# First expert's opening products in two interleaved sums, and table reads ahead of weight loads

## The chip, the core and the metric

The kernel runs on one core of one Trainium2 chip. The metric is the device time of one execution in microseconds (us); less is better. The engines are named as in the profile: PE (TensorE, with PEld for its weight loads), DVE (VectorE), ACT (ScalarE), POOL (GpSimd) and SP (SyncE, whose DMA queue is shown as SPq).

## The reference: what is computed

A linear attention with decay runs over 768 steps for 4 x 8 heads. Its rows, put together as 3072 tokens of 512 values, go through a layer of 8 experts, of which each token takes one.

```python
for t in range(S):                                   # S = 768, D = 64
    state = gamma * state + einsum('bhd,bhe->bhde', k[:, :, t], v[:, :, t])
    y[:, :, t] = scale * einsum('bhd,bhde->bhe', q[:, :, t], state)
x = y.transpose(0, 2, 1, 3).reshape(3072, 512)
...
logits = xn @ en.T / tau                             # xn, en: rows of length one
expert_idx = argmax(logits, axis=1)
gate_w = softmax(logits)[n, expert_idx]
for e in range(8):
    mask = expert_idx == e
    h = maximum(x[mask] @ w1[e], 0.0)                # 512 -> 1024
    out[mask] = gate_w[mask, None] * (h @ w2[e])     # 1024 -> 512
```

## The kernel before

**The attention part** walks over 12 chunks of 256 tokens (`m` from 0 to 11). In a chunk PE makes the scores and products, `take(m)` has ACT copy the result out of the two PSUM banks `py0` and `py1` into `yT` (one copy for `py0`, two half copies for `py1`), `rows_turn` and `rows` turn it into token rows and write them to DRAM (`xd`), and `logits_products`, `sums` and `choose` find each token's expert. `count`, `ranks` and `place` give every token a place in the table `tbl` in DRAM: `place` is one indirect DMA on POOL for each block of 128 tokens. The chunks are placed in groups; the last two groups are chunks 9 and 10, and chunk 11.

**The expert part** starts with the first 288 tokens of expert 0 (`EARLY`), which are known before chunk 11 is done. They are gathered as rows (`xge`), transposed by PE in 12 transposes (four column blocks `kt`, three row groups each) into four PSUM banks, and split into two float32r parts: `xh0`, rounded by ACT, and `xl0`, the rest, by DVE. Weights are split in the same way: `load_piece` issues the load of one piece of 512 KB (eight to an expert) on SP's queue into one of four `raw` buffers, `split` has ACT write `whi` and DVE `wlo`, each with nine buffers. Each product of the first layer is then three matmuls: `xh` by `whi`, `xl` by `whi`, `xh` by `wlo`. `products` is a generator that gives one matmul of expert 0's first layer at a time, so that `run(n)` puts n of them between other steps. The accumulators come from `acc_`, which goes round the PSUM banks in a fixed order, and the other results from `pt_`, which goes round b0 to b3:

```python
return bank(("py0", "py1", "pst0", "pst1", "b0", "b1")[nacc[0] % 6])
```

So the accumulator of the first output block is the bank `py0`, that of the second is `py1`, the same two that `take(11)` copies from.

**The rest of expert 0 and expert 1.** The 128 late tokens of expert 0 and the rows of expert 1 can be gathered only once all tokens are placed. SP reads their table entries into `tb` (the statement for `tb[:, 0, 3]` and `slots(1)`), POOL gathers (`xr`), `write_rows(1)` writes expert 1's rows to DRAM (`xs`) and `read_quarters(1)` reads them back in another layout (`xg`), from which `x_turn(1, kt)` (DVE transpose, ACT rounding) and `x_low(1, kt)` (DVE) make expert 1's `xh` and `xl`. Beside that PE works on expert 0's second layer, on the late tokens' products (`hr`), on their transposes (`turn_hidden`) and second layer (`layer2_rows`), and then begins expert 1. `split` calls stand between these steps.

**Order.** The instructions of all engines run in the order in which the program writes them (a manual schedule): every engine, and SP's queue, is a list worked off from its head, and a wait holds up all that stands behind it on that engine. The pools add waits where a buffer or bank is taken again.

Of the kernel before, what the change touches and what calls it, by code (L numbers as in the profile page):

```python
# [11 lines left out]
F32 = mybir.dt.float32  # L12
# [12 lines left out]
P = 128  # L25
# [80 lines left out]
def retention_moe(ctx: ExitStack, tc: tile.TileContext, q, k, v, emb, tau, w1, w2, const, const16, out):  # L106
# [503 lines left out]
    def turn_rows(xr, jn, kt, ps=None):  # L610
        ps = pt_() if ps is None else ps
        for c, (j, n) in enumerate(jn):
            nc.tensor.transpose(ps[:, c * P:c * P + n], xr[:n, j, kt * P:(kt + 1) * P], ident[:n, :n])
        return ps

    def rows_T(xr, jn, kt, at, ps=None):

        ps = turn_rows(xr, jn, kt) if ps is None else ps
        w = at.stop - at.start
        nc.scalar.copy(out=xh0[:, kt, at], in_=ps[:, :w])  # L620
        nc.vector.tensor_tensor(out=xl0[:, kt, at], in0=ps[:, :w], in1=xh0[:, kt, at].bitcast(F32), op=ALU.subtract)  # L621
# [139 lines left out]
    for m in range(NM):  # L761
# [61 lines left out]
        else:  # L823
# [39 lines left out]
            else:  # L863
# [4 lines left out]
                for low in lows:  # L868
                    low()
                intra(m, 1)  # L870
                pr = count(done)
                ps = [turn_rows(xge, EROWS, kt, bank(f"pst{kt}")) for kt in range(2)]
                run_all(ranks(done, pr))
                place(range(span(done).start, span(done).stop))
# [9 lines left out]
        if m == NM - 1:  # L884
            for kt in range(KT):
                rows_T(xge, EROWS, kt, slice(0, EARLY), ps[kt] if kt < 2 else None)
# [11 lines left out]
    def products():  # L898
        for ft in range(FT):
            acc = acc_()  # L900
            yield from first_layer(0, ft, acc, xh0, xl0, early)
            hidden(ft, acc, hh0, hl0, early, held if ft < 2 else None)
# [12 lines left out]
    m, g = NM - 1, len(GROUPS) - 1  # L915
    pl = logits_products(m)
# [4 lines left out]
    run(11)  # L921
# [13 lines left out]
    low()  # L935
    for _ in range(9):
        next(sort_steps)
        run(1)
    load_expert(1)
    load_piece()  # L940
    run(10)
    split()
    load_piece()
    load_expert(2)
    nc.sync.dma_start(out=tb[:, 0, 3], in_=tbl[EARLY:CAPS[0], :2 + NE])
    slots(1)
    slots(2)
    run(12)
    split()
    for j, n in EROWS:  # L950
        square(xge, n, j, j)
    run(12)
    split()
    load_piece()
    load_piece()
# [157 lines left out]
    write_rows(1)  # L1113
    hr = mp.tile([P, DF], F32, name="hr")
# [14 lines left out]
    load_piece()  # L1129
    load_piece()  # L1130
# [16 lines left out]
    squares(1, 1)  # L1147
    load_piece()
# [211 lines left out]
```

## Time and profile before

| what | value |
| --- | --- |
| time, median of 3 runs (lowest to highest) | 409.28 us (408.39 to 411.97) |
| profiled execution: time | 409.33 us |
| profiled execution: span from first to last instruction | 407.6 us |
| PE busy | 392.3 us, 96% of the span |
| DVE, ACT, POOL busy | 62%, 52%, 38% of the span |
| mean granted PE clock | 0.986 |
| DMA | 88.39 MB, mean 217 GB/s |

The span is 1.7 us shorter than the time of the same execution; sums in spans are carried to the time by adding this. A PE that is busy 96% of the span says where to look for the few stretches in which it isn't, not that each matmul is at its peak.

### The profile page before, as it was taken

To read this page: it belongs to the slowest core of one execution; us is meant where nothing else is said; L and a number is where in the kernel's file an instruction comes from. 1 tells how busy PE (TensorE), PEld (TensorE's weight loads), DVE (VectorE), ACT (ScalarE), POOL (GpSimd) and SP (SyncE) were. 2 spreads that over 40 slices of the span, in tenths; PEclk is the share of its full clock that TensorE was granted. 3 is DMA by queue.
4 is the path that set the end of the run, shared out by engine and by line. 5 is a ranking of instruction groups with operands and counts; after the bars stand their busy time and mean duration, and the time that the engine had idled before them with its cause. 6 is when DMAs were issued, how large, how long until landed. Compare 5 with 4: busy or idle time off the path is not lost.

```text
span 407.6 us, 9526 instructions
## 1 busy us (share of the span) xinstructions
PE 392.3 (96%) x3646; PEld 359.1 (88%) x3646; DVE 254.2 (62%) x539; ACT 213.5 (52%) x378; POOL 154.8 (38%) x170
## 2 busy tenths in 40 slices
PE   7999999999899999999999999999999999999993
PEld 3998788878687998899999999999889889999972
DVE  5496877767489847871963676396266465586400
ACT  4565566545484627543745644565475365563410
POOL 2666477676333270701631330261274062000040
PEclk9999999999799999999999999999999999999997
DMA  8998979888437978879596896888969958934121
GB/s 233 266 291 255 270 218 261 238 220 245 112 81 189 277 233 198 282 222 276 187 297 166 254 301 197 233 280 248 257 242 329 206 183 247 247 127 126 32 98 53
DMA packets 88479, 88.39 MB, mean 217 GB/s; under 512 B 10808, under 2 KB 67000, under 8 KB 88424
## 3 DMA queue, kind: packets, MB, share of 16 engines
q1 hardware_dynamic: 83176, 74.60, 64.5%
q0 software_dynamic: 5072, 13.03, 9.4%
q8 instruction: 30, 0.49, 0.5%
q14 instruction: 25, 0.20, 0.1%
q10 hardware_dynamic: 176, 0.07, 0.1%
HBM read 65.01 MB, written 18.79 MB: 206 GB/s over the span
## 4 chain that ended last, share of the span: by engine, by line
PE 76%; DVE 6%; issue 6%; DMA 5%; SPq 4%; POOL 1%; ACT 1%; POOLq 0%; DVEq 0%; ACTq 0%
PE pst L237 11%; PE b L237 9%; PE py L237 8%; PE py L1030 8%; PE b L1030 6%; PE pst L1030 6%; PE py L444 5%; PE b L381 5%; PE b L1078 4%; PE py L1078 4%; PE pst L415 2%; SPq L1042 2%; PE b L350 2%; DMA tbl<-parts 2%; DVE x L468 2%
## 5 line engine op out<-in xcount | busy, mean ns | idle before, releaser
L224 DVE TENSOR_TENSOR wlo<-raw,whi 128x1024 fp32r<-128x1024 f32 x64 | 77.8, 1219 | 21.0 <-ACT whi L219 13.6
L1060 POOL DMA_INDIRECT out_dram<-og,si x28 | 30.4, 1086 | 125.1 <-ACT og L1053 88.7
L219 ACT CAST whi<-raw 128x1024 fp32r<-128x1024 f32 x64 | 66.2, 1044 | 2.1 <-DMA raw<-in_moe_w_dram 2.1
L1011 DVE STREAM_TRANSPOSE xt<-xg 128x384 f32<-128x384 f32 (+1 forms) x28 | 15.7, 579 | 34.1 <-DMA xg<-xs 33.9
L596 POOL DMA_INDIRECT xr<-xd,gi x24 | 29.9, 1244 | 17.2 <-ACT sq L278 9.9
L401 DVE TENSOR_TENSOR pm<-b,mask 128x512 f32<-128x512 f32 x48 | 29.8, 681 | 9.1 <-PE b L381 9.1
L344 POOL TENSOR_TENSOR hl<-wlo,cst 128x512 f32<-128x512 f32 x22 | 22.7, 1051 | 32.9 <-DMA wlo<-in_k_dram 20.9
L237 PE MATMUL pst<-xl,whi 128*128 128x380 f32 (+7 forms) x96 | 32.1, 335 | 0.2 <-issue 0.2
L237 PE MATMUL pst<-xh,whi 128*128 128x380 f32 (+7 forms) x96 | 32.0, 334 | 0.0
L237 PE MATMUL pst<-xh,wlo 128*128 128x380 f32 (+7 forms) x96 | 32.0, 333 | 0.0
L566 POOL DMA_INDIRECT tbl<-zt,sloti x24 | 24.4, 1018 | 19.2 <-DVE sloti L557 8.9
L381 PE MATMUL b<-qT,kT 64*128 64x128 f32 x384 | 27.9, 283 | 2.9 <-issue 2.0
L1012 ACT CAST xh<-xt 128x408 fp32r<-128x408 f32 (+6 forms) x28 | 14.3, 510 | 28.4 <-DVE xt L1011 27.4
L381 PEld LDWEIGHTS b<-qT,kT 64*128 64x128 f32 x384 | 24.0, 187 | 5.6 <-issue 3.8
L237 PE MATMUL py<-xl,whi 128*128 128x288 f32 (+7 forms) x80 | 26.3, 328 | 0.5 <-DVE xl L621 0.5
L237 PE MATMUL b<-xh,whi 128*128 128x408 f32 (+7 forms) x80 | 26.7, 334 | 0.0
L237 PE MATMUL b<-xl,whi 128*128 128x408 f32 (+7 forms) x80 | 26.7, 333 | 0.0
L237 PE MATMUL b<-xh,wlo 128*128 128x408 f32 (+7 forms) x80 | 26.6, 332 | 0.0
L237 PE MATMUL py<-xh,whi 128*128 128x288 f32 (+7 forms) x80 | 26.3, 329 | 0.0
L237 PE MATMUL py<-xh,wlo 128*128 128x288 f32 (+7 forms) x80 | 26.2, 328 | 0.0
L444 PE MATMUL py<-pm,vs 128*64 128x128 f32 x384 | 24.3, 277 | 0.3 <-DVE vs L394 0.3
L243 ACT ACTIVATE hh<-pst 128x380 fp32r<-128x380 f32 (+7 forms) x24 | 11.6, 484 | 23.8 <-PE pst L237 23.1
(222 smaller groups left out, 1036.5 us busy)
## 6 DMA issues: line engine op xcount, KB each, us to landing
raw<-in_moe_w_dram SPq DMA_DIRECT2D x60, 512.0 KB
whi<-in_q_dram SPq DMA_DIRECT2D x24, 256.0 KB
xd<-x SPq DMA_DIRECT2D x48, 128.0 KB
wlo<-in_k_dram SPq DMA_DIRECT2D x11, 512.0 KB
xs<-xr SPq DMA_DIRECT2D x6, 768.0 KB
whi<-in_v_dram SPq DMA_DIRECT2D x6, 512.0 KB
wlo<-in_v_dram SPq DMA_DIRECT2D x6, 512.0 KB
xg<-xs SPq DMA_DIRECT2D x16, 192.0 KB
```

Of the source, the lines that this page charges most:

```text
L219: nc.scalar.copy(out=hv, in_=rv)
L224: eng.tensor_tensor(out=lv, in0=rv, in1=hv.bitcast(F32), op=ALU.subtract)
L237: nc.tensor.matmul(acc[:, :w], a[:, f], x[:, kt, cols], start=(n == 0), stop=(n == 3 * KT - 1))
L344: return eng.tensor_tensor(out=ks_r[:, m % 3, s, h], in0=kin[m % 3][:, h, s], in1=w[:, h], op=ALU.mult)
L381: nc.tensor.matmul(psc[a][:, j], kTs[m][a * D:(a + 1) * D, j, u].rearrange("p s c -> p (s c)"), q_cols(m, a, j, u), start=True, stop=True, ...
L401: o.append(nc.vector.tensor_tensor(out=pm, in0=psc[a], in1=w, op=ALU.mult))
L444: nc.tensor.matmul(pys[m][u][o * D:(o + 1) * D, j], lhsT, rhs, start=first, stop=True, skip_group_check=True)
L566: i = nc.gpsimd.indirect_dma_start(out=tbl[:, :], out_offset=bass.IndirectOffsetOnAxis(ap=sloti[:, n:n + 1], axis=0), in_=zt[:, n], in_off ...
L596: return nc.gpsimd.indirect_dma_start(out=xr[:n, j, :], out_offset=None, in_=xd[:rows_, :], in_offset=bass.IndirectOffsetOnAxis(ap=gi[:n, ...
L1030: nc.tensor.matmul(acc[:, :c], a[:, f], x[:, kt, :c], start=(n == 0), stop=(n == 3 * FT - 1))
L1060: i = nc.gpsimd.indirect_dma_start(out=out[:, :], out_offset=bass.IndirectOffsetOnAxis(ap=si[:n, e, j:j + 1], axis=0), in_=og[:n, j, :], i ...
L1078: nc.tensor.matmul(acc[:s, :], x[:, kt, at], a, start=(n == 0), stop=(n == 3 * FT - 1))
```

## The change: what it does

Four things are changed together, between the end of chunk 11 and the start of expert 1.

1. **Transposes and copies.** The 12 transposes of `xge` go row group by row group over all four banks, ahead of `count`, and the four roundings to `xh0` are put on ACT ahead of `take(11)`. On DVE the four subtractions to `xl0` now come ahead of the last `wlo` and of `ranks`, so that `place` of that group follows them.
2. **Products.** The first two output blocks of expert 0 are summed side by side, matmul by matmul, in the order all `xh` by `whi`, all `xl` by `whi`, all `xh` by `wlo`. Twelve of these 24 matmuls come ahead of the logits of chunk 11.
3. **Table reads.** On SP the reads of `tb` for expert 0's late tokens and for expert 1 come ahead of the weight load beside them, the squares of `xge` come earlier on ACT, and three splits of expert 0's weights are spread evenly.
4. **Weight loads.** Of expert 1's pieces (8 to 15) one is loaded where four were; piece 9 follows `write_rows(1)`, pieces 10 to 12 follow `read_quarters(1)`, 13 to 15 come later.

```diff
-    def turn_rows(xr, jn, kt, ps=None):
-        ps = pt_() if ps is None else ps
+    def turn_rows(xr, jn, ps):
         for c, (j, n) in enumerate(jn):
-            nc.tensor.transpose(ps[:, c * P:c * P + n], xr[:n, j, kt * P:(kt + 1) * P], ident[:n, :n])
-        return ps
-
-    def rows_T(xr, jn, kt, at, ps=None):
-
-        ps = turn_rows(xr, jn, kt) if ps is None else ps
-        w = at.stop - at.start
-        nc.scalar.copy(out=xh0[:, kt, at], in_=ps[:, :w])
-        nc.vector.tensor_tensor(out=xl0[:, kt, at], in0=ps[:, :w], in1=xh0[:, kt, at].bitcast(F32), op=ALU.subtract)
+            for kt in range(KT):
+                nc.tensor.transpose(ps[kt][:, c * P:c * P + n], xr[:n, j, kt * P:(kt + 1) * P], ident[:n, :n])
+
+    def rows_high(kt, at, ps):
+        nc.scalar.copy(out=xh0[:, kt, at], in_=ps[:, at])
+
+    def rows_low(kt, at, ps):
+        nc.vector.tensor_tensor(out=xl0[:, kt, at], in0=ps[:, at], in1=xh0[:, kt, at].bitcast(F32), op=ALU.subtract)
...
-                for low in lows:
-                    low()
+                lows.pop(0)()
                 intra(m, 1)
+                ps = [bank(f"pst{kt}") for kt in range(2)] + [pt_(), pt_()]
+                turn_rows(xge, EROWS, ps)
                 pr = count(done)
-                ps = [turn_rows(xge, EROWS, kt, bank(f"pst{kt}")) for kt in range(2)]
-                run_all(ranks(done, pr))
-                place(range(span(done).start, span(done).stop))
+                for kt in range(KT):
+                    rows_high(kt, slice(0, EARLY), ps[kt])
         waiting = done
         take(m)
...
         if m == NM - 1:
             for kt in range(KT):
-                rows_T(xge, EROWS, kt, slice(0, EARLY), ps[kt] if kt < 2 else None)
+                rows_low(kt, slice(0, EARLY), ps[kt])
+            lows.pop(0)()
+            run_all(ranks(done, pr))
+            place(range(span(done).start, span(done).stop))
...
     def products():
-        for ft in range(FT):
+        accs = [acc_(), acc_()]
+        for i in range(3):
+            for kt in range(KT):
+                x = xl0 if i == 1 else xh0
+                for ft, acc in enumerate(accs):
+                    nc.tensor.matmul(acc[:, :EARLY], piece[kt][i // 2][:, ft * P:(ft + 1) * P], x[:, kt, early],
+                                     start=(i + kt == 0), stop=(i == 2 and kt == KT - 1))
+                    yield
+        for ft, acc in enumerate(accs):
+            hidden(ft, acc, hh0, hl0, early, held)
+        for ft in range(2, FT):
             acc = acc_()
             yield from first_layer(0, ft, acc, xh0, xl0, early)
-            hidden(ft, acc, hh0, hl0, early, held if ft < 2 else None)
+            hidden(ft, acc, hh0, hl0, early)
...
     m, g = NM - 1, len(GROUPS) - 1
+    run(12)
     pl = logits_products(m)
     logits_rows(m, pl)
     rows(m - 1)
     load_piece()
     load_piece()
-    run(11)
+    run(6)
...
     low()
+    for j, n in EROWS:
+        square(xge, n, j, j)
     for _ in range(9):
         next(sort_steps)
         run(1)
+    nc.sync.dma_start(out=tb[:, 0, 3], in_=tbl[EARLY:CAPS[0], :2 + NE])
     load_expert(1)
-    load_piece()
-    run(10)
-    split()
+    slots(1)
     load_piece()
     load_expert(2)
-    nc.sync.dma_start(out=tb[:, 0, 3], in_=tbl[EARLY:CAPS[0], :2 + NE])
-    slots(1)
     slots(2)
-    run(12)
-    split()
-    for j, n in EROWS:
-        square(xge, n, j, j)
-    run(12)
-    split()
-    load_piece()
-    load_piece()
+    for _ in range(3):
+        run(12)
+        split()
...
     write_rows(1)
+    load_piece()
...
     read_quarters(1)
-    load_piece()
-    load_piece()
+    for _ in range(3):
+        load_piece()
...
     squares(1, 1)
+    load_piece()
     load_piece()
```

On ACT, where chunk 11 ends (`yT` is copied from `py`, `xh` from the banks of the transposes, `whi` is a weight split), the order before is:

```order
L219 CAST whi<-raw 128x1024 x2
L460 COPY yT<-py_2082 128x4x128
L463 COPY yT<-py_2083 64x4x128 x2
L620 CAST xh<-pst_2173 128x288
L620 CAST xh<-pst_2177 128x288
L620 CAST xh<-b_2205 128x288
```

and now it is:

```order
L219 CAST whi<-raw 128x1024 x2
L616 CAST xh<-pst_2166 128x288
L616 CAST xh<-pst_2167 128x288
L616 CAST xh<-b_2168 128x288
L616 CAST xh<-b_2169 128x288
L460 COPY yT<-py_2082 128x4x128
```

The copies that empty `py` (2082 and 2083 are the two banks of chunk 11) have moved from ahead of the four `xh` copies to behind them.

On PE, at the same place, the order before is (`pst` and `b` are the transposes' banks, `enT` the logits, `py_2237` the accumulator of the first output block):

```order
L613 MATMUL b_2205<-ident,xge 128x32
L613 MATMUL b_2211<-ident,xge 128x128 x2
L613 MATMUL b_2211<-ident,xge 128x32
L488 MATMUL b_2219<-yT,enT 32x256 x4
L237 MATMUL py_2237<-xh,whi 128x288
L237 MATMUL py_2237<-xl,whi 128x288
L237 MATMUL py_2237<-xh,wlo 128x288
```

and now it is, with the last matmul of `count` at its head (`py_2219` and `py_2220` are the two accumulators):

```order
L537 MATMUL b_2182<-oh,ones 128x8
L905 MATMUL py_2219<-xh,whi 128x288
L905 MATMUL py_2220<-xh,whi 128x288
...
L905 MATMUL py_2220<-xl,whi 128x288
L488 MATMUL b_2233<-yT,enT 32x256 x4
L905 MATMUL py_2219<-xl,whi 128x288
```

Twelve products, which go to both banks in turn, now stand ahead of the logits, and the transposes and `count` ahead of them.

On SP's queue, from the table reads to expert 1's rows, the order before is (`raw` are weight loads, `xs` the rows written, `xg` the rows read back):

```order
L945 DMA tb<-tbl 128x10
...
L913 DMA tb<-tbl 128x4x10
...
L194 DMA raw<-in_moe_w_dram 128x1024
L194 ISA
L194 DMA raw<-in_moe_w_dram 128x1024
L982 DMA xs_66<-xr 128x512
```

and now it is:

```order
L992 DMA xs_66<-xr 32x512
L194 ISA
L194 DMA raw<-in_moe_w_dram 128x1024
L1007 DMA xg<-xs_66 32x13x128
...
L194 ISA
L194 DMA raw<-in_moe_w_dram 128x1024
L194 ISA
L194 DMA raw<-in_moe_w_dram 128x1024
```

The loads of pieces 9, 10 and 11 have moved from ahead of expert 1's row writes to behind them, piece 9 in front of the reads `xg` and the other two behind these.

## Rows read from the trace of the kernel before

**Rows 1.** Page, part 1: busy time, share of the span, instructions.

```profile
PE 392.3 (96%) x3646; PEld 359.1 (88%) x3646; DVE 254.2 (62%) x539; ACT 213.5 (52%) x378; POOL 154.8 (38%) x170
```

**Rows 2.** What PE waited for, 130:376: us, times, longest.

```profile
PE pst L237 <- issue: 0.2, 1, 0.2
```

**Rows 3.** Timeline of PE around chunk 11's end: start, us, what, idle before.

```profile
121.94 0.19 PE L533 MATMUL b<-cum,ones 128*128 128x32 f16 x1
...
122.30 1.14 PE L613 MATMUL pst<-ident,xge 128*128 128x128 f32 x6
...
124.45 0.64 PE L488 MATMUL b<-yT,enT 128*32 128x256 f32 x8
125.02 0.40 PE L237 MATMUL py<-xh,whi 128*128 128x288 f32 x1
125.93 0.40 PE L237 MATMUL py<-xl,whi 128*128 128x288 f32 x1 [0.51 <-DVE xl L621]
126.17 0.29 PE L237 MATMUL py<-xh,wlo 128*128 128x288 f32 x1
126.30 0.29 PE L237 MATMUL py<-xh,whi 128*128 128x288 f32 x1
```

**Rows 4.** Timeline of ACT, same place.

```profile
121.19 0.58 ACT L460 COPY yT<-py 128x512 f32<-128x512 f32 x1
122.06 1.17 ACT L463 COPY yT<-py 64x512 f32<-64x512 f32 x2 [0.29 <-PE py L444]
123.25 0.70 ACT L620 CAST xh<-pst 128x288 fp32r<-128x288 f32 x2
124.01 0.94 ACT L620 CAST xh<-b 128x288 fp32r<-128x288 f32 x2
```

**Rows 5.** Timeline of DVE, same place.

```profile
122.63 2.36 DVE L224 TENSOR_TENSOR wlo<-raw,whi 128x1024 fp32r<-128x1024 f32 x2
...
125.42 0.81 DVE L621 TENSOR_TENSOR xl<-pst,xh 128x288 fp32r<-128x288 f32 x2
```

**Rows 6.** Stretches of 1.5 us: length, PE busy (instructions), granted clock, DMA share, GB/s.

```profile
103.50:105.00 1.50, 0.59 (x5) 1.00 0.83 224
...
106.50:108.00 1.50, 1.50 (x28) 0.50 0.14 38
...
112.50:114.00 1.50, 1.50 (x12) 0.76 0.00 0
```

**Rows 7.** Timeline of POOL: gathers for expert 0's late tokens and expert 1.

```profile
143.90 1.16 POOL L596 DMA_INDIRECT xr<-xd,tb  x1 [4.59 <-DMA tb<-tbl]
...
145.68 1.11 POOL L596 DMA_INDIRECT xr<-xd,gi  x1 [0.28 <-POOL gi L590]
```

**Rows 8.** Timeline of SP's queue: start of the issue, us, what.

```profile
137.48 1.00 SPq L194 DMA_DIRECT2D raw<-in_moe_w_dram  x2
...
140.98 0.99 SPq L194 DMA_DIRECT2D raw<-in_moe_w_dram  x2
149.39 3.65 SPq L982 DMA_DIRECT2D xs<-xr  x3
...
155.99 1.88 SPq L1001 DMA_DIRECT2D xg<-xs  x4
158.07 4.53 SPq L198 DMA_DIRECT2D raw<-in_moe_w_dram  x4
```

**Rows 9.** Stretches of 2 us, PE, PEld, DVE, ACT, POOL busy, clock, DMA share, GB/s.

```profile
160.00:162.00 2.00, 2.00 (x10) 1.60 (x9) 1.75 (x3) 1.97 (x4) 0.00 (x0) 1.00 1.16 210
162.00:164.00 2.00, 2.00 (x10) 1.63 (x9) 1.76 (x4) 1.34 (x4) 0.93 (x1) 1.00 1.04 386
```

**Rows 10.** Timeline of ACT: the split of piece 10.

```profile
157.77 1.07 ACT L219 CAST whi<-raw 128x1024 fp32r<-128x1024 f32 x1
```

**Rows 11.** Timeline of DVE: expert 1's first transposes.

```profile
162.34 1.10 DVE L1011 STREAM_TRANSPOSE xt<-xg 128x416 f32<-128x416 f32 x2
```

**Rows 12.** Timeline of PE: expert 1's first products.

```profile
166.40 0.46 PE L237 MATMUL pst<-xl,whi 128*128 128x408 f32 x1 [0.16 <-issue]
```

## The prediction

> **What bounds the kernel now.** I read the page first: PE is busy for 392.3 us of 407.6 [rows 1]. Then the list of PE's waits by stretch: from 130 to 376 us the profile shows one, of 0.2 us [rows 2]. From the first expert on PE is a closed chain, so whatever holds it up there moves the end by as much, and whatever frees another engine moves nothing. Then the timeline of PE where chunk 11 ends. `count` begins at 121.94, the 12 transposes take from 122.30 to 124.45, the logits from there to 125.02, and the first product follows at once. The second begins only at 125.93, after a wait of 0.51 for `xl`, and from 126.17 on there is a matmul each 0.13 us [rows 3]. The part of the change that works on products has this hole to win, some 0.8 us with its restart. Last I read the same place on ACT, where `py0` and `py1` are copied out from 121.19 to 123.23, before `xh` [rows 4], and on DVE, where two weight splits of 2.36 together stand ahead of `xl` [rows 5].
>
> **The opening products.** The transposes take `count`'s place at 121.94 and last 2.15, to 124.09; `count` with its 0.36 comes behind them and ends at 124.45, where the transposes ended before. Nothing is won or lost on PE by that. But now the row groups go round over the four banks, so no bank is whole before the last third of the transposes, the four short ones. The first `xh` copy, at 123.25 before, can then start at about 123.9. Four copies in a row, at the 0.70 that two take, end at about 125.3 (124.95 before) [rows 4].
>
> The price is what stands behind them. `take(11)` is now behind the four copies on ACT: 0.58 for `py0` and 1.17 for `py1` [rows 4] end at 125.9 and 127.05, not at 123.23. `acc_` begins its round with `py0` and `py1`, so the first product waits for the one copy, the second for the other, and PE works in order. So PE stands still from 124.45 to 125.9, does one product, and stands again to 127.05. Before, the second product began at 125.93, which is 1.12 earlier, and the logits, 0.57 [rows 3], were already done; now they come behind twelve products. Since all else is the same number of matmuls, PE is 1.12 + 0.57 = 1.7 us late from here on. The hole of 0.51 for `xl` is gone in this sum: one weight split less ahead of it lets `xl` begin at about 124.4, long before its first use. Bounds: with the first copy at 123.25 as before, the chain ends at 126.4 and PE is 1.0 late; with the copies at 0.94 for two [rows 4] it ends at 127.6, and PE is 2.2 late. I take 1.7.
>
> On DVE the logits' transpose followed the four `xl` subtractions at about 126.9 (125.42 and two pairs of 0.81, overlapping a little [rows 5]). Now it follows the logits, which begin at 127.05 + 11 x 0.13 = 128.5 and end at 129.1. Everything that hangs on it, `choose`, `ranks` and the last `place`, is about 2.3 us later, the 2.3 being 129.2 less 126.9. The wait of DVE costs nothing by itself, but the gathers of expert 1 wait for that `place`.
>
> **The table reads.** Before, they stood behind two weight loads issued at 137.48 [rows 8], of 0.5 MB each, so 2.7 us at the 386 GB/s that loads reach [rows 9], and behind some 1.2 us of issues. Expert 0's late gather waited for its read until 143.90, and expert 1's first started at 145.68 [rows 7]. That gain of up to 3.9 less the 2.3 of the later `place` is 1.6; I take the gathers as 1.5 earlier, with ends of 2.7 earlier (a smaller loss) and 1 later (a smaller gain). On PE nothing waits for these gathers before `turn_late`, and no wait of PE is shown there [rows 2], so this alone is worth nothing; it pays only through the next step. The squares moved on ACT and the even splits fall in stretches where PE doesn't wait, and cost nothing.
>
> **The weight loads.** Before, pieces 10 and 11 were issued at 140.98, the rows of expert 1 written from 149.39 and read back from 155.99, and four further loads issued from 158.07 [rows 8]. Piece 10 was split at 157.77 [rows 10], long after it had landed. Now pieces 9 to 11 are issued behind the writes `xs`, 10 and 11 also behind the four reads `xg`. With gathers 1.5 earlier, `xg` is issued at 154.5. Before, the queue moved 210 GB/s until 162 and 386 behind that [rows 9]: the reads of short rows first, then the loads. So the reads took until about 161.3, 5.3 us from their issue, and now until 159.8. Piece 9 goes into the pause between `xs` and `xg` and costs them nothing, by my choice; if it doesn't fit, it costs 1.4. Piece 10 needs 0.52 MB at 386 GB/s, 1.4 us: it lands at 161.2. PE's delay would have allowed its split at 157.77 + 1.7 = 159.5.
>
> From the split of piece 10 to the first transpose of expert 1's rows was 162.34 - 157.77 = 4.6 us [rows 10, 11] of splits, copies for the late tokens and squares in ACT's and DVE's order, with about 0.5 of waiting in it. From 161.2 that gives 161.2 + 4.1 = 165.3, which is 3.0 later than 162.34. PE has no slack towards this chain: it already waited at 166.40 for the third column block [rows 12]. So PE is then 3.0 late and not 1.7; the 1.7 is within the 3.0 and isn't added. Bounds: 1.3 if the loads come in time and the little hole at 166.40 closes (1.7 less 0.4), 4.4 if piece 9 delays the reads by its 1.4. I take 3.0, since three of the four terms are rows of this queue.
>
> How two transfers of one queue share the engines decides between 1.7 and 3.0. The rates of rows 9 show the reads going first. The Trainium skill, "DMA: Bandwidth & Descriptors", section "Queues, rings and completion order", says that each DMA engine takes the descriptors of a queue in the order in which they were put there. By that the load of piece 10 stands behind all of `xg`, as in the sum; with the two side by side it would land in time and the sum would be the second rival's 411.0.
>
> **Sum.** 409.33, the profiled execution's own time, which is 0.05 above the median of the runs, + 3.0 = **412.3 us**, 0.7% slower. Less than 1% either way is about what a measurement of this kernel can't tell from no change.
>
> **The rivals.**
>
> *The clock falls.* The granted clock fell to 0.50 of full, 1.2 of 2.4 GHz, just before 106.50, after a stretch in which PE was busy for 0.59 of 1.5 us, and came back within 112.50 to 114.00 [rows 6], so it was low for some 6.8 us. Now PE stands still for some 2.4 us between 124.45 and 127.05. If the clock falls behind that, products at half pace lose 1.7 us in 3.4 us and 3.4 in 6.8. PE would be 1.7 + 1.7 = 3.4 to 5.1 late, the late weights hidden behind it: 412.7 to 414.4, say 413.8. For it speaks that the hole is longer than any in that stretch; against it that the work on both sides is denser.
>
> *The loads are hidden, and only the opening waits.* Then PE is 1.7 late: 411.0. For it speaks that DMA is not full between 144 and 158 and that the reads may come earlier than I have them; against it the queue's order.
>
> *The change does what it is meant to.* If PE found `py0` and `py1` empty at 124.45, the second product would begin at 124.6 and not at 125.93, less 0.57 for the logits: 0.8 won, 408.6 with loads in time. The point from which it decides is whether the copies of `py` end before 124.45. Against it stands ACT's order; there is nothing for it but that a wait is inferred here and not seen.
>
> *The late weights hold up more.* Piece 9 late as well (its split stands ahead of the gates and of the late tokens' copies on ACT), or the reads slower: 4.4 to 6 late, 413.7 to 415.3.
>
> **How the numbers follow.** Forecast 0.42, clock 0.22, hidden loads 0.18, as meant 0.10, later weights 0.08. Slower than 413.4 are two thirds of the clock's cases, all of the last and a little of the forecast's: 0.26. Faster than 405.2 is none of these; 0.02 for what I don't see. The rest, 0.72, is within 1%. The range goes from 409.0, which leaves out most of the cases as meant, to 414.6, which leaves out half of the last.
>
> **What would show it.** In the profile after, PE's second product should begin near 127.0 with an ACT copy of `yT` as releaser, and the logits behind twelve products. ACT should be idle from 121.3 to about 123.9. The split of piece 10 should be released by its DMA at about 161, and expert 1's first transpose start at about 165.3. A granted clock below 1.00 between 124 and 136 would show the first rival. I am wrong if the `py` copies end before 124.5, or if expert 1's transposes start no later than PE's own delay explains.

## The result, and the profile after

| | median of the runs | lowest to highest |
| --- | --- | --- |
| before, 17 runs beside those of the changed kernel | 408.72 us | 404.97 to 412.45 |
| changed kernel, 17 runs | 413.26 us | 410.92 to 416.17 |
| ratio | 1.0115 | 95% interval 1.0093 to 1.0137 |

The change costs 4.5 us. Ratios, here and below, are taken from runs within 1.5% of the fastest of their kernel, so they can differ a little from those of the medians. The profiled execution took 411.63 us, 1.6 less than the median of its runs, with a span of 409.8 us and a mean granted clock of 0.994 (the median of the 17 runs is 0.989). Part 1 of its page answers [rows 1]: PE is as busy as before.

```profile
PE 392.0 (96%) x3646; PEld 358.0 (87%) x3646; DVE 254.1 (62%) x539; ACT 213.6 (52%) x378; POOL 150.2 (37%) x170
```

What PE waited for between 119 and 180 us, where before there was one entry of 0.2 [rows 2] (us in all, times, longest):

```profile
PE py L905 <- ACT yT L460: 1.5, 1, 1.5
PE pst L1084 <- DVE hl L1146: 1.1, 2, 0.9
PE py L905 <- ACT yT L463: 0.8, 1, 0.8
PE b L1143 <- ACT hr L1130: 0.8, 1, 0.8
PE pst L237 <- DVE xl L1024: 0.6, 2, 0.3
```

The first and the third are the copies out of `py`, the other three are late tokens and expert 1. The timeline of PE at the end of chunk 11 answers [rows 3]:

```profile
118.14 1.09 PE L444 MATMUL py<-pm,vs 128*64 128x128 f32 x16
119.17 0.44 PE L613 MATMUL pst<-ident,xge 128*128 128x128 f32 x2
...
120.56 0.19 PE L533 MATMUL b<-cum,ones 128*128 128x32 f16 x1
...
122.32 0.40 PE L905 MATMUL py<-xh,whi 128*128 128x288 f32 x1 [1.49 <-ACT yT L460]
123.52 1.20 PE L905 MATMUL py<-xh,whi 128*128 128x288 f32 x7 [0.80 <-ACT yT L463]
...
125.18 0.64 PE L488 MATMUL b<-yT,enT 128*32 128x256 f32 x8
```

The transposes take 1.39 (119.17 to 120.56) and not 2.15; then PE stands for 1.49, does one product and stands for 0.80. The timeline of ACT shows why (answering [rows 4]), and further down the splits of pieces 9 and 10 (answering [rows 10]):

```profile
120.47 0.70 ACT L616 CAST xh<-pst 128x288 fp32r<-128x288 f32 x2 [1.90 <-PE pst L613]
121.06 0.72 ACT L616 CAST xh<-b 128x288 fp32r<-128x288 f32 x2
121.64 0.63 ACT L460 COPY yT<-py 128x512 f32<-128x512 f32 x1
122.29 1.17 ACT L463 COPY yT<-py 64x512 f32<-64x512 f32 x2
...
153.88 1.05 ACT L219 CAST whi<-raw 128x1024 fp32r<-128x1024 f32 x1 [2.15 <-DMA raw<-in_moe_w_dram]
157.68 0.58 ACT L1130 ACTIVATE hr<-py 128x512 f32<-128x512 f32 x1
158.16 0.58 ACT L1145 CAST hh<-b 128x512 fp32r<-128x512 f32 x1
160.63 1.05 ACT L219 CAST whi<-raw 128x1024 fp32r<-128x1024 f32 x1 [1.90 <-DMA raw<-in_moe_w_dram]
161.59 0.58 ACT L1145 CAST hh<-b 128x512 fp32r<-128x512 f32 x1
```

ACT was idle for 1.90 with `py` full, because the four `xh` copies stood at its head. Later it waited for a weight twice, for piece 9 with `hr` behind it and for piece 10 with the second `hh` behind it. The queue of SP that brought them (start of the issue, answering [rows 8]):

```profile
149.70 0.32 SPq L992 DMA_DIRECT2D xs<-xr  x1
150.32 0.34 SPq L194 DMA_DIRECT2D raw<-in_moe_w_dram  x1
151.58 2.00 SPq L1007 DMA_DIRECT2D xg<-xs  x4
153.80 0.93 SPq L194 DMA_DIRECT2D raw<-in_moe_w_dram  x2
154.92 10.15 SPq L198 DMA_DIRECT2D raw<-in_moe_w_dram  x4
```

and DVE's first transpose of expert 1 (answering [rows 11]):

```profile
164.59 1.10 DVE L1017 STREAM_TRANSPOSE xt<-xg 128x416 f32<-128x416 f32 x2
```

The two profiles reach the end of chunk 11 at different times (120.92 before, 118.14 now; the clock, which before was back only between 112.50 and 114.00 [rows 6], is back at 108 now). So I count the stages below from the start of the last 16 attention products of chunk 11, the first row of the timeline of PE above. They are starts of matmuls in the timeline of PE; the last column is the rest of the span.

| kernel | third output block of expert 0 | `hr` | transposes of `hr` | `layer2_rows` | expert 1 | to the end |
| --- | --- | --- | --- | --- | --- | --- |
| before | 8.56 | 28.64 | 34.22 | 38.21 | 43.87 | 286.68 |
| changed | 9.70 | 29.81 | 35.58 | 40.65 | 48.12 | 291.66 |
| later by | 1.14 | 1.17 | 1.36 | 2.44 | 4.25 | 4.98 |

The opening makes 1.14 of it; from `hr` to expert 1 another 3.1 come, and 0.7 more inside expert 1's first block. From there on nothing is lost or won. (4.98 less the 2.78 by which the chunk ended earlier is the 2.2 between the two spans.)

### The profile page after: what moved, and what is told of

It is laid out like the page before. It is cut to its first block, busy times and chain, and to the rows that moved or that the text cites. A ratio compares the mean times of both kernels' runs of the same rounds, so it can differ in the third digit from the quotient of the medians.

```text
span 409.8 us, 9527 instructions
## 1 busy us (share of the span) xinstructions
PE 392.0 (96%) x3646; PEld 358.0 (87%) x3646; DVE 254.1 (62%) x539; ACT 213.6 (52%) x378; POOL 150.2 (37%) x170
## 4 chain that ended last, share of the span: by engine, by line
PE 68%; DMA 10%; issue 6%; DVE 6%; SPq 4%; POOL 2%; ACT 2%; POOLq 0%; DVEq 0%; ACTq 0%
PE pst L237 10%; PE b L237 8%; PE py L1036 7%; PE py L237 7%; PE py L444 6%; PE b L1036 5%; PE b L381 5%; PE pst L1036 4%; PE b L1084 4%; PE py L1084 4%; DMA xd<-x 3%; SPq L1048 2%; PE pst L415 2%; PE b L350 2%; DMA raw<-in_moe_w_dram 2%
## 5 line engine op out<-in xcount | busy, mean ns | idle before, releaser
L1066 POOL DMA_INDIRECT out_dram<-og,si x28 | 29.4, 1050 | 121.5 <-ACT og L1059 86.1
L596 POOL DMA_INDIRECT xr<-xd,gi x24 | 28.6, 1193 | 20.4 <-issue 18.2
L263 POOL TENSOR_TENSOR r<-r,half 128x4 f32<-128x4 f32 (+1 forms) x9 | 8.9, 993 | 50.1 <-DVE r L262 50.1
L237 PE MATMUL py<-xh,whi 128*128 128x360 f32 (+7 forms) x72 | 23.8, 331 | 0.0
L237 PE MATMUL py<-xl,whi 128*128 128x360 f32 (+7 forms) x72 | 23.8, 331 | 0.0
```

The source lines that it names most:

```text
L237: nc.tensor.matmul(acc[:, :w], a[:, f], x[:, kt, cols], start=(n == 0), stop=(n == 3 * KT - 1))
L596: return nc.gpsimd.indirect_dma_start(out=xr[:n, j, :], out_offset=None, in_=xd[:rows_, :], in_offset=bass.IndirectOffsetOnAxis(ap=gi[:n, ...
L1066: i = nc.gpsimd.indirect_dma_start(out=out[:, :], out_offset=bass.IndirectOffsetOnAxis(ap=si[:n, e, j:j + 1], axis=0), in_=og[:n, j, :], i ...
```

## Experiments

Each group of four shared a chip and the runs of the kernel before on it. Its median there was 401.96 us for runs 1 to 4, 408.31 for runs 5 to 8 and 401.96 for runs 9 to 12. So only ratios are compared across groups, and the us in this table are the ratio's. The stages are those of one profile each, counted as above, and the kernel before has a profile on one chip only. In the profiles of runs 1 to 4 and 9 to 12 chunk 11 ends 5 to 8 us earlier in the span than in that one (the last attention products start at 112.65 to 115.66, not at 120.92). The next weight of expert 0 doesn't land earlier by as much, and ACT waits 3.4 to 5.9 us for it behind the `xh` copies, where it waits at most 1.8 in the others.

| run | ratio, 95% interval | us against before | third block | `layer2_rows` | expert 1 | to the end |
| --- | --- | --- | --- | --- | --- | --- |
| 1 opening alone | 1.0070 [1.0045, 1.0095] | +2.8 | 9.68 | 42.63 | 48.26 | 290.84 |
| 2 reads and loads alone | 1.0076 [1.0040, 1.0112] | +3.1 | 8.70 | 38.62 | 45.60 | 289.54 |
| 3 all, loads early | 1.0092 [1.0060, 1.0125] | +3.7 | 11.04 | 40.42 | 46.04 | 289.71 |
| 4 all, loads early, `py` first | 1.0031 [1.0013, 1.0050] | +1.2 | 8.09 | 38.33 | 44.30 | 288.33 |
| 5 all, `py` first | 1.0078 [1.0040, 1.0115] | +3.2 | 7.55 | 39.67 | 48.14 | 291.62 |
| 6 all, piece 9 early | 1.0151 [1.0092, 1.0209] | +6.2 | 11.15 | 40.69 | 49.83 | 292.41 |
| 7 opening, `py` and ranks first | 1.0021 [0.9982, 1.0060] | +0.9 | 7.55 | 39.77 | 45.43 | 287.99 |
| 8 as 7, reads first, loads early | 1.0001 [0.9964, 1.0039] | 0.0 | 7.55 | 37.12 | 43.46 | 287.46 |
| 9 all, splits behind `x_turn` | 1.0128 [1.0092, 1.0164] | +5.1 | 11.50 | 40.98 | 47.16 | 293.25 |
| 10 as 7, squares and splits moved | 1.0188 [1.0162, 1.0215] | +7.6 | 7.55 | 39.78 | 45.45 | 295.10 |
| 11 as 8, loads spread, splits moved | 1.0212 [1.0180, 1.0244] | +8.5 | 7.87 | 38.62 | 44.28 | 294.87 |

Run 12 was run once, for a row of its trace, and is not in the table.

**Run 1: the opening alone** (parts 1 and 2 of the change; table reads, squares and loads as before, so against the changed kernel):

```diff
-    for j, n in EROWS:
-        square(xge, n, j, j)
     for _ in range(9):
         next(sort_steps)
         run(1)
-    nc.sync.dma_start(out=tb[:, 0, 3], in_=tbl[EARLY:CAPS[0], :2 + NE])
     load_expert(1)
-    slots(1)
     load_piece()
+    run(10)
+    split()
+    load_piece()
     load_expert(2)
...
     write_rows(1)
-    load_piece()
```

> Only parts 1 and 2 of the change (transposes, copies, interleaved products); table reads and weight loads as before. Theory: the opening costs about 1.1 us through the wait for the copies of py0 and py1, and the late weights cost the rest, about 3.5. Then this kernel is 0.5 to 1.7 us above before, PE shows the two waits of 1.5 and 0.8 us for yT, and ACT waits for no weight load between 150 and 165. Rival (all of the loss starts in the opening, by the hole on PE and a clock that falls behind it): 3.5 to 4.5 us above before, with a granted clock below 1.00 between 122 and 134.

+2.8, between the two. The waits for `yT` are there, 1.5 and 0.8, and PE is 1.12 late at the third block, as in the changed kernel. The rest came elsewhere. ACT waited for a weight of expert 0, with the squares of `xge` behind that split and an `hh` behind the squares (timeline of ACT):

```profile
133.55 1.05 ACT L219 CAST whi<-raw 128x1024 fp32r<-128x1024 f32 x1 [2.61 <-DMA raw<-in_moe_w_dram]
...
136.64 0.38 ACT L243 ACTIVATE hh<-b 128x288 fp32r<-128x288 f32 x1
```

and a stretch behind it (us, then PE, PEld, DVE, ACT, POOL busy, clock, DMA share, GB/s):

```profile
140.00:144.00 4.00, 4.00 (x21) 4.00 (x20) 2.02 (x9) 0.00 (x0) 3.06 (x4) 0.57 0.84 250
```

PE then waited 0.9 for `hl`, and in the 4 us behind that the mean granted clock was 0.57. That profile is the longest of the run's twelve (408.21 with a median of 405.09), so the fall is hardly in all of them.

**Run 2: the reads and loads alone** (parts 3 and 4 in the kernel before, the reverse of the diff of run 1 applied to it).

> Only parts 3 and 4 of the change (table reads first, weight loads late); the opening as before. Theory: 2 to 4 us above before, since ACT waits for pieces 9 and 10 and PE for what ACT does behind them; somewhat less than in the whole change, because place, and with it the gathers, is not held up by the opening. Rival (loads are hidden, and the opening costs all): within 0.5 us of before.

+3.1, as the theory said. ACT waits for pieces 9 and 10 (its timeline):

```profile
146.58 1.05 ACT L219 CAST whi<-raw 128x1024 fp32r<-128x1024 f32 x1 [1.62 <-DMA raw<-in_moe_w_dram]
152.83 1.05 ACT L219 CAST whi<-raw 128x1024 fp32r<-128x1024 f32 x1 [1.40 <-DMA raw<-in_moe_w_dram]
```

and PE for what stands behind them (its waits):

```profile
PE pst L1072 <- DVE hl L1134: 0.8, 2, 0.5
```

So each half costs about 3 alone, and both together 4.5. The halves don't simply add: run 1 pays at the squares in their old place, which the whole change has moved (the changed kernel's profile has no wait for `hl` or `hh` there), and a PE that is late anyway can wait less for a late weight. How much each of these makes isn't separated.

**Run 3: the whole change with pieces 9 to 11 loaded right behind the table reads**, and one load less at each of the later places, as in the kernel before.

```diff
     slots(2)
+    for _ in range(3):
+        load_piece()
...
     write_rows(1)
-    load_piece()
```

> The whole change, but pieces 9, 10 and 11 are loaded right behind the table reads, ahead of the row writes, as many loads as before stand there. Theory: ACT no longer waits for a weight between 150 and 165, PE's waits for hr, hl and xl there go back to the one small one of before, and the time is 0.5 to 1.7 us above before. Rival (the reads of expert 1's rows, not the weights, are late): still 3 us or more above before, with the first transpose of expert 1 released by its DMA.

+3.7: the theory missed, and the rival's sign is there. No split of piece 9 or 10 waits for its load, and PE's waits for `hr` and `hl` are gone. But in this execution the clock fell behind the opening's hole (to 0.50, 1.2 of 2.4 GHz, between 118 and 120): seven products that take 1.20 in the changed kernel took 2.05 (PE's timeline):

```profile
118.32 2.05 PE L905 MATMUL py<-xh,whi 128*128 128x288 f32 x7 [0.80 <-ACT yT L463]
```

with the stretch of 4 us around them (columns as in run 1):

```profile
116.00:120.00 4.00, 2.07 (x8) 1.86 (x9) 2.87 (x8) 2.24 (x5) 0.78 (x1) 0.74 0.87 195
```

And DVE waited for the reads `xg`. With the three loads ahead of the rows' traffic these were issued 37.98 behind the start of the last attention products, against 33.44 in the changed kernel (DVE's timeline):

```profile
157.40 1.11 DVE L1019 STREAM_TRANSPOSE xt<-xg 128x416 f32<-128x416 f32 x2 [1.01 <-DMA xg<-xs]
```

**Run 4: run 3 with the `py` copies ahead of the `xh` copies.**

```diff
-                for kt in range(KT):
-                    rows_high(kt, slice(0, EARLY), ps[kt])
         waiting = done
         take(m)
+        if m == NM - 1:
+            for kt in range(KT):
+                rows_high(kt, slice(0, EARLY), ps[kt])
```

> As the kernel with the three loads put back, and the copies of py0 and py1 go ahead of the four roundings to xh on ACT. Theory: the roundings start no later than now, since ACT stood idle for 1.9 us ahead of them, the waits of 1.5 and 0.8 us on PE shrink to less than 0.5 together, and the time is 0.5 to 1.5 us below before. Rival (the opening is bound by the transposes or by xh, not by py): no better than with the loads put back alone.

+1.2, where the theory had a gain. The `yT` waits are gone and the run is 2.5 faster than run 3, which is the price of the copies' order with the falls of the clock behind it. It still isn't faster than the kernel before: DVE waits 1.66 for `xg`, and PE 0.6 for `rs`, a step of `ranks` on DVE. That one goes back to a weight of expert 0, behind which the first `hh` stands on ACT, and behind that `hl` and `rs` on DVE (ACT's timeline):

```profile
122.44 1.05 ACT L219 CAST whi<-raw 128x1024 fp32r<-128x1024 f32 x1 [5.31 <-DMA raw<-in_moe_w_dram]
```

**Run 5: the whole change with that one edit**, loads as late as in the change.

> The whole change with one edit: the copies of py0 and py1 stand ahead of the four xh copies again. Theory (hole and late weights are two costs in a row; the logits, place, the row writes and so the loads behind them all move forward with PE): the yT waits of PE are gone, the second product begins 1.5 us earlier, and of the changed kernel's +4.5 against the kernel before +2.0 to +3.2 is left, the late weights alone. Rival (the late weights alone set the start of expert 1, the hole lies inside their wait): +4.0 to +5.0, with a longer wait for piece 9.

+3.2, the top of the theory's span, but its interval (1.6 to 4.7 us) reaches into the rival's and overlaps the changed kernel's, so the time decides nothing. PE is 1.0 ahead of the kernel before at the third block (7.55 against 8.56) and has lost it again before `hr`, by a wait for `rs` of 1.3 and what follows. Expert 1 starts at 48.14, as late as in the changed kernel with its hole (48.12). So in this profile the late weights set the start of expert 1 whether PE is late or early, as the rival had it, though it is piece 10 that ACT waits longer for, and not piece 9. The largest of PE's waits, the reads on SP's queue, and the split of piece 10 on ACT:

```profile
PE b L237 <- DVE rs L553: 1.3, 1, 1.3
...
153.31 1.88 SPq L1008 DMA_DIRECT2D xg<-xs  x4
...
163.60 1.05 ACT L219 CAST whi<-raw 128x1024 fp32r<-128x1024 f32 x1 [2.90 <-DMA raw<-in_moe_w_dram]
```

**Run 6: the whole change, piece 9 right behind the table reads.**

```diff
     slots(2)
+    load_piece()
...
     write_rows(1)
-    load_piece()
```

> The whole change with the load of piece 9 issued right behind the table reads; pieces 10 to 12 as late as in the change. Theory (piece 9, which I had costed at nothing, holds ACT 2.15 us at the head of expert 0's late tokens, and is most of what the sum was short of): ACT waits for a weight once and not twice, PE's waits for hr and hl (1.1 and 0.8) are gone, and it is 1.0 to 2.0 us faster than the changed kernel: +2.5 to +3.5 against the kernel before. Rival (piece 10, behind the reads xg, sets expert 1's transposes whatever piece 9 does): +4.0 to +5.0, the ACT wait for piece 10 growing by what the other one loses.

+6.2: the theory fell. The wait for `hr` is gone, but piece 10 makes up for it, with a longer wait (ACT's timeline):

```profile
163.03 1.05 ACT L219 CAST whi<-raw 128x1024 fp32r<-128x1024 f32 x1 [3.59 <-DMA raw<-in_moe_w_dram]
```

behind the reads (SP's queue):

```profile
154.70 1.88 SPq L1008 DMA_DIRECT2D xg<-xs  x4
```

From the issue of `xg` to that split are 8.3 us, against 9.05 in the changed kernel. In the profile of this run two other things made it slower still: the clock fell behind the hole (third block at 11.15, not 9.70) and again behind the wait for piece 10, to 0.67 in the mean between 168 and 172.

**Run 7: the opening with the `py` copies, `ranks` and `place` first**; reads and loads as before (the edits of runs 1 and 4, and this one).

```diff
                 pr = count(done)
+                run_all(ranks(done, pr))
+                place(range(span(done).start, span(done).stop))
...
             lows.pop(0)()
-            run_all(ranks(done, pr))
-            place(range(span(done).start, span(done).stop))
```

> The kernel before with the changed transposes and the two interleaved sums alone: the copies of py0 and py1 ahead of the xh copies, ranks and place as early as before, table reads and loads as before. Theory (the interleaved sums do win the hole for xl of 0.5 us and its restart, and the transposes round the four banks another 0.7, when nothing is put ahead of the py copies): no yT wait on PE, -0.5 to -1.5 us. Rival (expert 1's start is set by its rows and not by PE, so what PE wins is given back as a wait there): -0.3 to +0.5, with a new wait of PE or DVE for xg or piece 10 before expert 1.

+0.9, not to be told from no change, and nearer to the rival. The opening is 1.0 us shorter, as meant. At the weight split with the squares behind it this is given back, as in run 1, and 1.3 more (`hr` at 29.90, not 28.64): PE waits for `hl` 0.9 and for `hh` 0.5. The rival's own sign, a wait for `xg` or piece 10, isn't there.

**Run 8: run 7 with the table reads first and the loads of run 3.**

> As the run with the py copies first and ranks and place early, with the table reads ahead of the loads of pieces 9 to 11, which are all issued right behind these reads. Theory (the late rows of the run with early loads and py first came from its late place; with place early again the gathers and xs run ahead of PE's need): no wait for xg, -0.5 to -1.5 us. Rival (three loads in a row ahead of the rows' traffic on SP's queue delay xg whenever place comes): +0.5 to +1.6, with x_turn waiting for xg again.

0.0, between the two by its time (its interval, 1.5 us either way, reaches both), and as the rival said by its trace. PE reaches `layer2_rows` 1.1 us earlier than in the kernel before and then stands for expert 1's rows (DVE's timeline):

```profile
162.37 1.11 DVE L1020 STREAM_TRANSPOSE xt<-xg 128x416 f32<-128x416 f32 x2 [2.03 <-DMA xg<-xs]
```

**Run 9: the whole change, the splits of pieces 10 and 11 behind `x_turn`.**

```diff
     turn_hidden(0)
-    split()
...
     turn_hidden(1)
-    split()
...
     x_low(1, 0)
+    split()
     x_turn(1, 2)
     x_low(1, 1)
+    split()
```

> The whole change, loads as late as in it, but the splits of pieces 10 and 11 stand behind x_turn(1, 0), x_turn(1, 1) and x_low(1, 0) on ACT and DVE, not ahead of them and of the second turn_hidden. Theory (the late piece 10 costs what it does because hl of the late tokens and x_turn stand behind its split, while expert 1 needs that piece only at its third column block): PE's wait for the second hl is gone, x_turn starts on the landing of xg, 6.5 to 6.8 us behind its issue, and the run is 1.5 to 3.0 us faster than the changed kernel: +1.5 to +3.0 against the kernel before. Rival (expert 1 needs the piece as soon as its first products run, so the order makes no difference): +4.0 to +5.0, with PE waiting for whi or wlo in expert 1's first block.

+5.1, as much as the rival said, for another reason. The wait for the second `hl` fell from 0.88 to 0.2 and `x_turn` began earlier. But the splits now stand between the four transposes, and ACT and DVE wait for each other in turn, 3.3 us a step; PE waited 2.0 for `xl` inside the first block, and the clock fell behind that (0.59 in the mean from 164 to 168). It also fell in the opening (third block at 11.50).

**Run 10: run 7 with the squares of `xge` ahead of the sort steps and the splits as in run 9.**

> As the run with py first, ranks early and the loads of the kernel before, with two moves on ACT and DVE: the squares of xge stand ahead of the sort steps, and the splits of pieces 10 and 11 behind x_turn. Theory (that run lost its 1.3 us of the opening in the waits for hh and hl, 1.4 in all, and then in x_turn behind two splits): neither wait, x_turn starts some 40.7 us behind the last intra and not 41.4 as in the kernel before, and it is 0.4 to 1.2 us faster than the kernel before. Rival (the reads xg land no earlier, or another wait takes the place): -0.2 to +0.6.

+7.6: a clear miss, by the same placing of the splits. The squares did what was expected (no wait for `hh` or `hl`). But PE waited 1.1 for `rs`, behind a weight of expert 0 as in run 4, and stood 1.3 ahead of the late tokens' transposes, so that `hr` came at 30.22 and not at 28.64. The reads came at 43.85 (158.85 less 115.00) and not at 40.7, and PE waited twice inside the first block, with the clock low behind it (PE's timeline):

```profile
163.77 0.45 PE L237 MATMUL pst<-xl,whi 128*128 128x408 f32 x1 [2.25 <-DVE xl L1031]
...
167.06 0.71 PE L237 MATMUL pst<-xl,whi 128*128 128x408 f32 x1 [2.47 <-DVE xl L1031]
```

and the stretch there (columns as in run 1):

```profile
164.00:168.00 4.00, 1.53 (x6) 1.17 (x6) 3.07 (x5) 2.19 (x3) 0.00 (x0) 0.59 0.60 197
```

**Run 11: run 8 with piece 9 behind the reads, 10 in the pause between `xs` and `xg`, 11 to 13 behind `xg`, splits as in run 9.**

> py first, ranks early, table reads first, piece 9 behind them, 10 between the row writes and the reads, 11 to 13 behind xg, and the splits of pieces 10 and 11 behind x_turn. Theory (one load in place of three ahead of the gathers brings xg 1 us forward against the run with three; nothing in front of x_turn waits for a weight): -0.4 to -1.5 us against the kernel before. Rival (piece 10 in the pause holds up xg by its 1.4, or pieces 10 and 11 come too late for the first block): 0 to +1.5, with a wait of x_turn for xg or of PE for wlo.

+8.5, mostly by the splits again (PE waits 3.6 for `xl` inside the first block, and 7.8 of the loss come behind the start of expert 1), so this says nothing of the loads' places as a whole. It gives one number: with a load in the pause, `xg` landed 7.8 us behind its issue (SP's queue):

```profile
148.85 2.00 SPq L1009 DMA_DIRECT2D xg<-xs  x4
```

and DVE's timeline:

```profile
156.68 1.11 DVE L1019 STREAM_TRANSPOSE xt<-xg 128x416 f32<-128x416 f32 x2 [1.14 <-DMA xg<-xs]
```

Where none stood there and DVE waited for `xg`, it was 6.5 in run 3, 6.7 in run 4, 6.8 in run 8, 6.9 in run 10 and 6.5 in run 12.

**Run 12: run 7 with the twelve transposes bank by bank**, all other things as there.

```diff
-        for c, (j, n) in enumerate(jn):
-            for kt in range(KT):
+        for kt in range(KT):
+            for c, (j, n) in enumerate(jn):
```

> The run with py first, ranks early and the loads of the kernel before, with the 12 transposes bank by bank as in the kernel before (three row groups of one bank, then the next), all twelve together. One look at the trace. If the order of the row groups sets what the twelve take, they take about 2.15 us as in the kernel before, not 1.39; if it was the split into two groups of six, about 1.4.

The first six waited for `xge` itself, which spoils their sum; the six of the other two banks, without a wait, took 1.08 (117.61 to 118.69), as each six did before [rows 3], against 0.70 for a half of the 1.39. So it is the order of the row groups. PE's timeline:

```profile
117.61 1.16 PE L613 MATMUL b<-ident,xge 128*128 128x128 f32 x6
118.69 0.19 PE L533 MATMUL b<-cum,ones 128*128 128x32 f16 x1
```

## Why the prediction was right, and where its sizes were off

The sign, the range and both mechanisms held: 412.3 was forecast and 413.26 measured. That the two lie so close is partly luck. The sum had +3.0 and the change costs +4.5; 0.6 of that difference doesn't show, since the kernel before ran at 408.72 beside it and not at the 409.33 from which I started. By its stages the changed kernel's profile is 4.98 late, which is the rival of the later weights (4.4 to 6, for piece 9 late or the reads slower; both were), to which I gave 0.08. And the times that I named as signs, 161 for the split of piece 10 and 165.3 for the first transpose, were nearly met (160.63 and 164.59) only because chunk 11 ended 2.78 earlier than before. By its steps:

**The opening.** PE stood for the two `yT` copies, the logits came behind twelve products, and ACT was idle ahead of them, all as written. PE was 1.14 late at the third block, where I took 1.7 with bounds of 1.0 and 2.2. The step that was off is "The transposes take `count`'s place at 121.94 and last 2.15": they took 1.39, so the first `xh` copy came 2.33 behind the start of the last attention products and not 2.98.

**The table reads.** I took the gathers as 1.5 earlier. Counted from the same start they were 0.55 earlier (expert 1's first at 142.35 less 118.14, 24.21, against 24.76 [rows 7]); `xg`, on which the next step rests, was issued 1.63 earlier (33.44 against 35.07 [rows 8]), where the sum had 1.5. The squares cost nothing in the changed kernel's profile. PE's waits for `rs` in other runs aren't theirs where the trace shows the cause: in runs 4, 10 and 11 ACT stood 5.3 to 5.9 for a weight of expert 0, with `hh` behind it, and the squares came only after that `hh`. What held DVE in run 5 (1.3) stays open.

**The late weights.** Here the sum was short. Expert 1's first transpose started 5.0 later than before (46.45 against 41.42 behind the same start), not 3.0. From the issue of `xg` to the split of piece 10 I had 6.7 (161.2 less 154.5); it was 9.05 (160.63 less 151.58). From that split to the transpose it was 3.96, with 4.1 forecast. So the whole miss, 2.3 less these small gains, lies in the queue. Two terms of the sum were too small:

- "5.3 us from their issue" for the reads: where DVE waited for them with no load in front, 6.5 to 6.9 (runs 3, 4, 8, 10 and 12). I had taken the end of the reads from the rate of the whole queue [rows 9], which isn't when the last of them has landed. That is 1.2 to 1.6 more than the sum had, in five profiles.
- "Piece 9 goes into the pause between `xs` and `xg` and costs them nothing, by my choice; if it doesn't fit, it costs 1.4": in the one profile that shows the landing with a load in the pause (run 11), the reads took 7.8, which is 0.9 to 1.3 more. Piece 9 itself was late too, by 2.15 on ACT, which PE paid with 0.8 for `hr` and 0.2 for `hl`.

How these add up to the miss isn't shown. From the issue of `xg` to the split of piece 10 it was 9.05 here, 8.2 in run 2 (152.83 less the 144.61 below) and 10.3 in run 5 (163.60 less 153.31), all with piece 9 in the pause, and 8.3 without it in run 6. So one order of the queue gave values 2 us apart, as much as the terms themselves, and the 1.4 for the load of piece 10 can be neither confirmed nor refuted. Moving piece 9 alone gains nothing (run 6). SP's queue in run 2:

```profile
144.61 1.94 SPq L995 DMA_DIRECT2D xg<-xs  x4
```

The rates tell why a load so late can't be sized by its bytes. Stretches of 2 us in the changed kernel (columns of run 1):

```profile
152.00:154.00 2.00, 2.00 (x12) 1.59 (x11) 0.00 (x0) 0.12 (x1) 0.20 (x1) 1.00 0.83 282
154.00:156.00 2.00, 2.00 (x17) 2.00 (x16) 1.04 (x1) 1.97 (x4) 0.00 (x0) 1.00 0.92 187
156.00:158.00 2.00, 1.52 (x12) 1.28 (x10) 1.52 (x11) 0.77 (x4) 0.00 (x0) 1.00 1.28 223
158.00:160.00 2.00, 1.46 (x7) 1.05 (x8) 1.04 (x3) 0.73 (x2) 0.00 (x0) 1.00 0.96 320
```

From 152 to 160 us 2.02 MB were moved. Piece 9, the four reads of 208 KB and piece 10 together are 1.90, and piece 10 was still not there. An estimate from this, which no view shows directly: pieces that stand behind it had already begun on engines that had done their share. The Trainium skill, "DMA: Bandwidth & Descriptors", section "Queues, rings and completion order", on which the prediction weighed its choice, speaks of an order within one engine's queue; the trace agrees in that the rate stays near 200 while the reads are under way and rises behind them, and shows that this order doesn't give the time at which one transfer is whole.

**The clock.** In the changed kernel's profile it stayed at 1.00 (2.4 GHz) through the hole, with PE busy for 0.88 of 2 us:

```profile
122.00:124.00 2.00, 0.88 (x4) 0.67 (x5) 1.96 (x5) 1.43 (x3) 0.00 (x0) 1.00 0.98 305
```

The rival was still real: of the five profiles with this hole it stayed through the opening in two (changed kernel, run 1) and fell there in three (runs 3, 6 and 9). In these the third block began at 11.04 to 11.50 and not at 9.70, so a fall costs 1.3 to 1.8 where I had worked out 1.7 to 3.4. How many of the 17 timed runs had it, no record shows. But their mean granted clock is 0.989 in the median, against 0.994 in the profile, and on another chip that of run 3 is 0.988, against 0.996 for run 4, which differs from it by the copies' order alone. So part of the 4.5 may be a fallen clock, which the stages of this one profile don't contain; how much stays open.

**The change as meant.** Its copies were the obstacle, as forecast: with `py` first the third block is at 7.55, 1.0 earlier than before (0.8 was worked out). That this agrees is luck too. The transposes are 0.76 shorter, which the sum had at nothing, and that leaves an estimate of 0.25 for the interleaved sums. Run 12, with the old order of the transposes, has the third block at 9.34; without its two waits for `xge` (0.46 and 0.37) that would be 8.5, as before. And no run turned the 1.0 into time. In runs 4 and 8 the rows of expert 1 came too late, in run 7 a weight of expert 0 held ACT, and in run 5 PE waited for `rs` and then for what stands behind piece 10. No kernel here beat the one before; run 8 comes level with it, within 0.4% either way.

## What to carry to other kernels

Before a copy is put behind others on an engine that works in order, look up which bank it empties and who takes that bank next: here the next product did. A load that is moved behind other traffic has to be sized from its issue to the landing that releases its reader, in a row where something waited for it, since a queue's rate only bounds that from below (here 5.3 by the rate and 6.5 to 6.9 to the landing). And a hole that is closed pays only as far as what comes next is early: the 1.0 us won in the opening went to a weight in run 7 and to the rows of expert 1 in run 8.

## What the runs showed of the hardware that I had not expected

The order of the transposes' shapes costs PE time. The weight loads before, bank by bank (timeline of PEld; the size behind LDWEIGHTS and the names is the tile):

```profile
122.28 0.20 PEld L613 LDWEIGHTS pst<-ident,xge 128*128 128x128 f32 x2
122.64 0.38 PEld L613 LDWEIGHTS pst<-ident,xge 32*128 32x128 f32 x3 [0.17 <-issue]
```

and the transposes now, row group by row group (timeline of PE):

```profile
119.88 0.38 PE L613 MATMUL b<-ident,xge 128*128 128x128 f32 x2
120.19 0.31 PE L613 MATMUL pst<-ident,xge 32*128 32x32 f32 x2
```

Bank by bank, the tile goes from 128*128 to 32*128 and back in each bank, with 0.17 of idle time ahead of each of the four changes to 32*128; row group by row group there is one such change, and the same twelve take 1.39 and not 2.15. The six transposes that run 12 shows without a wait, in the old order, take as long as before, so it is the order; whether going round the banks has a part in it, beside the tile, isn't separated. The Trainium skill, "TensorEngine Tiling (Array Packing)", section "Key Properties", says that changing the tiling mode drains TensorE; the trace agrees, and over the six changes saved (seven before, one now) it comes to an estimate of 0.13 us for each. Taken into account ahead, this would have told that the term of the opening is smaller than 2.15, though not by how much.
